# Splitting the ring of h: fifteen slots for loaded parts, six for rounded ones

## The chip, the cores and the metric

The kernel runs on one core of a Trainium2 chip. The metric is device time in microseconds (us) of one execution. The core has five engines, each with an instruction queue of its own that is worked in order: TensorE (PE, with its weight loads as PEld), VectorE (DVE), ScalarE (ACT), GpSimd (POOL) and SyncE (SP), which here only issues DMA transfers. An instruction that waits for a semaphore holds up everything behind it on its engine.

## The reference

A retention layer gives x, and a mixture of eight experts with dense weights is applied to it. Cut to the core:

```python
def _attn_ref(q, k, v):                       # 4 x 8 heads, 768 steps, 64 wide
    for t in range(S):
        state = gamma[None, :, None, None] * state + einsum('bhd,bhe->bhde', k[:, :, t], v[:, :, t])
        y[:, :, t] = scale * einsum('bhd,bhde->bhe', q[:, :, t], state)

def _moe_ref(x, w_gate, w1, w2):              # x: 3072 x 512, 8 experts, F = 1024
    logits = x @ w_gate
    P = exp(logits - logits.max())
    for _ in range(8):
        P /= P.sum(1, keepdims=True) + 1e-09
        P /= P.sum(0, keepdims=True) + 1e-09
        P *= N / E
    for e in range(E):
        h = maximum(x @ w1[e], 0.0)
        out += P[:, e:e + 1] * (h @ w2[e])
```

All arrays are float32.

## The kernel before, in words

The products of the experts are done with Strassen's scheme at one level, in the form that needs seven products M1 to M7 for a 2 by 2 block product. Each float32 operand is split into two parts that TensorE takes at full rate: a rounded value ("hi", made by ScalarE, `hi_act`, line 77) and the remainder ("lo", a subtraction on VectorE or GpSimd, line 80). A product is then three matmuls: hi x hi, lo x hi, hi x lo.

Three pieces of work follow one another.

*Retention* (up to about 145 us) gives x, written to `xd` in device memory.

*Stage 1* (x @ w1, matmuls on line 190) is 96 units of class `UnitA`: 32 pieces of w1 by three pieces of x. A unit is seven products of six matmuls. The loop goes through the units by `ROW`, seven places m = 0 to 6: M6 of unit n, M1 of n+1, M3 and M7 of n, M2 and M5 of n+1, M4 of n. `post` takes each product out of PSUM (lines 207 to 229), and the seven combinations of h that stage 2 needs (after the relu) are stored to `hd` (line 200). Line 213 is M3's sum on VectorE; M5 of the next unit uses the same PSUM bank and waits for it. Below, row 94 and row 95 are the last two turns of this loop (`n == NUA - 2` and `n == NUA - 1`). Units 93, 94 and 95 are the last users of three buffers of split w1, `WA`, each 7 slots of 512 columns.

*Stage 2* (h @ w2, matmuls on line 540) is 24 units of class `UnitB`: eight experts by three pieces of x. A product is cut into four quarters, so there are 24 x 7 x 4 = 672 parts, numbered s. Part s needs one piece of 128 x 512 of h: `h_load(s)` loads it from `hd` on SyncE's queue (line 600), `h_conv(s)` splits it (ScalarE rounds, VectorE subtracts in place, lines 605 and 606), and `b_part(s)` issues its six matmuls, then the work that follows the product (`post`, on every fourth part), a load, the split of part s+5 and, on three parts of four, one task from a list that prepares the next expert's w2 (`w2_tasks`: four subtractions on GpSimd on line 641, three roundings, three remainders, twice for each expert). M2, M3, M7 and M4 end in `emit` (lines 549 to 558): VectorE combines and scales the output, and a DMA takes it out; from the second expert on GpSimd issues that DMA, which adds to `out`.

The loaded and split parts live in a ring `HR` in the three `WA` buffers, which are free by then: nine slots of 1024 columns, the first half for hi, the second for the loaded value, which becomes lo. Part s uses slot s % 9:

```python
HR = [WA[(len(jobs) - 3 + k) % 3]....[:, i * 1024:(i + 1) * 1024]
      .rearrange("p (h t) -> p h t", h=2) for k in range(3) for i in range(3)]
```

In stage 2 `b_part(s)` issues the load of part s+9 behind the matmuls of part s, which free its slot. At the change of stage the loads of parts 0 to 2 stand at the start of row 94, those of 3 to 5 at the start of row 95, and those of 6 to 8 behind unit 95; `b_part(4)` adds those of 9 to 12. Parts 0 to 3 are computed inside row 95: 0 and 1 behind M6, 2 and 3 behind M7.

The order on each engine is the order in which the program issues the instructions; there is no planner.

Of the kernel before, what the change touches and what calls it, by code (L numbers as in the profile page):

```python
# [18 lines left out]
P = 128  # L19
# [18 lines left out]
M1, M2, M3, M4, M5, M6, M7 = range(7)  # L38
# [3 lines left out]
XP = {M1: 0, M2: 1, M3: 2, M7: 3, M5: 4, M6: 5, M4: 6}  # L42
# [5 lines left out]
def kernel(  # L48
# [17 lines left out]
    pe, act, dve, pool = nc.tensor, nc.scalar, nc.vector, nc.gpsimd  # L66
    sp = nc.sync
# [5 lines left out]
    def rd(t):  # L73
        return t.bitcast(F32)

    def hi_act(o, i):
        act.activation(o, i, AF.Copy)  # L77

    def lo(eng, o, full, h):
        eng.tensor_tensor(o, full, rd(h), ALU.subtract)  # L80
# [14 lines left out]
    X0 = cst.tile([P, 7, 2, 1024], F32R, name="X0")  # L95
    WA = [cst.tile([P, 7, 2, 256], F32R, name=f"WA{i}") for i in range(2)]
# [4 lines left out]
    hd = [[[drp.tile([P, QE, 512], F32, name=f"hd{e}_{r}_{i}") for i in range(7)] for r in range(NPAIR)] for e in range(E)]  # L101
    pd = drp.tile([NTILE * E, P], F32, name="pd")

    def run(q, n):
        for _ in range(min(n, len(q))):
            q.pop(0)()


    def x_load(t, r):
        for i, c, d in ((M1, 0, 0), (M7, 1, 0), (M3, 1, 1), (M2, 0, 1)):  # L110
            for k in range(2):
                sp.dma_start(rd(t[:, XP[i], 1, k * 512:(k + 1) * 512]).rearrange("p (b s) -> p b s", s=C),  # L112
                             xd[2 * r + c][:, :, 2 * d + k, :])
# [37 lines left out]
    def w1_load(n):  # L151
        sp.dma_start(w1_raw(n)[:, 0:4, :], w1[jobs[n]])
# [26 lines left out]
    class UnitA:  # L179
# [5 lines left out]
        def mm(self, i):  # L185
            ps = PS1[self.bank[i]]
            w, x = WA[self.job % 3][:, WP[i]], self.x[:, XP[i]]
            for k in range(2):
                for m, (a, b) in enumerate(((0, 0), (1, 0), (0, 1))):
                    pe.matmul(ps, w[:, a, k * P:(k + 1) * P], x[:, b, k * 512:(k + 1) * 512],  # L190
                              start=i in PRE and k == 0 and m == 0, stop=k == 1 and m == 2, **kw)
# [55 lines left out]
    jobs, first, last = {}, {}, {}  # L247
# [6 lines left out]
    with tc.manual_schedule():  # L254
        with ExitStack() as ph:
# [156 lines left out]
            for tau in range(2, NCHUNK):  # L412
                c, b = divmod(tau, B)
# [80 lines left out]
        def sink_t():  # L494
# [15 lines left out]
        NUA = len(UA)  # L510


        HR = [WA[(len(jobs) - 3 + k) % 3].rearrange("p s h c -> p (s h c)")[:, i * 1024:(i + 1) * 1024]
              .rearrange("p (h t) -> p h t", h=2) for k in range(3) for i in range(3)]
        NSH = len(HR)
        WB = [X1, X0]
        YS = [OT[:, 10:12, :], XSC[:, 0:2, :], XSC[:, 2:4, :]]
        TB = [OT[:, 2 * k:2 * k + 2, :] for k in range(3)]
# [3 lines left out]
        class UnitB:  # L522
# [12 lines left out]
            def mm(self, i, q, h):  # L535
                ps = self.bank(i)
                w = WB[(E - 1 - self.e) % 2][:, VP[i]]
                for d in range(2):
                    for m, (a, b) in enumerate(((0, 0), (1, 0), (0, 1))):
                        pe.matmul(ps[d] if isinstance(ps, tuple) else ps[:, d, :], w[:, a, q * 256 + d * P:q * 256 + d * P + P], h[:, b, :],  # L540
                                  start=i in PRE and q == 0 and m == 0, stop=q == QE - 1 and m == 2, **kw)

            def emit(self, c, dh, src, add):
# [53 lines left out]
        def h_load(s):  # L597
            if s < len(parts):
                u, i, q = parts[s]
                sp.dma_start(rd(HR[s % NSH][:, 1]), hd[u.e][u.r][i][:, q, :])  # L600

        def h_conv(s):
            if s < len(parts):
                t = HR[s % NSH]
                hi_act(t[:, 0], rd(t[:, 1]))
                lo(dve, t[:, 1], rd(t[:, 1]), t[:, 0])

        w2x = RW.rearrange("p (s c) -> p s c", s=7)

# [46 lines left out]

        bq = []

        def b_part(s):
            u, i, q = parts[s]  # L660
            if i == M6 and q == 0 and u.n + 1 < len(UB):
                UB[u.n + 1].load_p()
            u.mm(i, q, HR[s % NSH])
            if q == QE - 1:
                u.post(i)
            if s == 4:
                for x in range(NSH, NSH + 4):
                    h_load(x)
            if s >= 4:
                h_load(s + NSH)  # L670
                h_conv(s + 5)
            e, g = divmod(u.n, NPAIR)
            if q != 1:
                run(bq, 1)
            if g == 0 and i == M6 and q == 0 and e + 1 < E:
                bq.extend(w2_tasks(e + 1, 0) + w2_tasks(e + 1, 1))
# [13 lines left out]
        for n, u in enumerate(UA):  # L690
            v = UA[n + 1] if n + 1 < NUA else None
            while conv < loaded and n >= first[conv] - 2 and n > last.get(conv - 3, -1):
                wq += w1_tasks(conv, pool, dve)
                conv += 1
            if n == NJ:
                x_load(X0, 2)
                xq = x_tasks(X0, [dve, pool])
            if n == 40:
                ps_s.close()
                ps_B = ctx.enter_context(tc.tile_pool(name="ps_B", bufs=1, space=PSUM, reuse_waits="tile"))  # L700
                PS2 = [ps_B.tile([P, 2, 512], F32, name=f"psB{i}") for i in range(2)]
            if n == NUA - 2:
                UB[0].load_p()
            if n >= NUA - 2:
                for s in range(3):
                    h_load(s + 3 * (n - NUA + 2))
            for m, (k, i) in enumerate(ROW):
                w = (u, v)[k]
                if w is not None:
                    w.mm(i)  # L710
                    w.post(i)
                if m == 0 and carry is not None:
                    carry.last_sum()
                if m == 4:
                    u.sums()
                if m in (0, 1, 5):
                    run(wq, 1)
                if m in (1, 6) or n >= NJ:
                    run(xq, 2 if n >= NJ else 1)
                for f, x in w2_plan.get((n, m), ()):  # L720
                    w2_first(f, x)
                if n == NUA - 2 and m in (1, 3, 6):
                    h_conv((1, 3, 6).index(m))
                if n == NUA - 1 and m in (0, 1):
                    h_conv(3 + m)
                if n == NUA - 1 and m in (0, 3):
                    b_part(0 if m == 0 else 2)
                    b_part(1 if m == 0 else 3)
            carry = u
            while loaded < len(jobs) and loaded <= conv + 1 and n + 1 >= first[loaded] - 3:  # L730
                w1_load(loaded)
                loaded += 1
            if 12 <= n < 12 + len(sink):
                sink[n - 12]()
        carry.last_sum()
        for s in range(6, NSH):
            h_load(s)
        for s in range(5, NSH):
            h_conv(s)
        for s in range(4, len(parts)):  # L740
            b_part(s)
# [51 lines left out]
```

## Time and profile before

| | |
|---|---|
| median of 3 runs | 2132.11 us (2131.82 to 2138.85) |
| the profiled execution | 2132.21 us |
| its span, first to last instruction | 2129.5 us |
| PE busy | 2015.4 us, 95% of the span |
| DVE, ACT, POOL busy | 1543.6, 1041.1, 497.3 us |
| mean granted TensorE clock | 0.982 |
| parts of h: loads | 672 of 256 KB, median 5.7 us from issue to landing |
| moved by DMA | 503.62 MB, mean 236 GB/s |

The profile is of one execution. A line of the timeline gives the start and length in us, the engine (SPq for a DMA that SyncE issues), the program's line, the operation, out<-in by the program's names, shapes, the count, and in brackets how long the engine had been idle and what ended that. A line of the groups gives busy time and mean ns, then the idle time before the group and its releasers. A line of the stretches gives the bounds, the length, the busy time with the count, the granted clock, the DMA engines' busy share and GB/s. The chain of waits is the work that ended last, followed back, each piece with start and length. Matmul ends are modelled: a matmul's record is longer than its share of the pipeline, so a pause on TensorE is better counted from the number of matmuls in a stretch than from idle time.

### The profile page before, as it was taken

The numbers are of one execution on the slowest core, as the hardware profiler recorded it, in microseconds if no ns is written. First come the engines' busy times: TensorE is split into PE (matmuls) and PEld (weight loads), VectorE is DVE, ScalarE is ACT, GpSimd is POOL, SyncE is SP. The second block draws the span as 40 slices with busy tenths as digits, with TensorE's granted clock in tenths as the row PEclk, the third lists the DMA queues.
The fourth block names the chain that finished last, engine by engine and source line by source line (L and its number), as shares of the span: only waits on it lengthen the run. The fifth ranks groups of instructions, "written<-read, shape, count | busy, mean of one in ns | idle before, by whom it ended". The sixth has DMA issues, their size and how long they took to land.

```text
span 2129.5 us, 28865 instructions
## 1 busy us (share of the span) xinstructions
PE 2015.4 (95%) x9273; PEld 1646.9 (77%) x9273; DVE 1543.6 (72%) x2025; ACT 1041.1 (49%) x1668; POOL 497.3 (23%) x479
## 2 busy tenths in 40 slices
PE   7788999998999999999998999999999999999997
PEld 6786877886788888888876777877878787777886
DVE  6795988986566666666665777779587777768765
ACT  3343554553444444444444545555464555555553
POOL 4462433332121111211221201212030212203001
PEclk9899999999999999999998999999999999999999
DMA  7755776775566666666666778999989999989987
GB/s 231 242 168 178 251 228 225 242 238 176 201 224 227 218 219 216 227 223 220 231 231 233 241 254 255 275 268 250 282 247 261 271 256 271 261 268 247 261 261 180
DMA packets 252906, 503.62 MB, mean 236 GB/s; under 512 B 27793, under 2 KB 40401, under 8 KB 250705
## 3 DMA queue, kind: packets, MB, share of 16 engines
q1 hardware_dynamic: 240656, 457.73, 63.9%
q0 software_dynamic: 12096, 44.05, 12.1%
q8 instruction: 72, 1.18, 0.2%
q14 instruction: 82, 0.66, 0.1%
HBM read 268.79 MB, written 232.88 MB: 236 GB/s over the span
## 4 chain that ended last, share of the span: by engine, by line
PE 65%; DVE 13%; DMA 10%; issue 7%; ACT 3%; SPq 1%; POOL 1%; DVEq 0%; POOLq 0%; ACTq 0%
PE psA L190 41%; PE psA L540 12%; PE psB L540 10%; DMA WA<-hd 7%; DVE WA L80 6%; DVE X L80 2%; DVE XSC L551 1%; ACT WA L77 1%; DVE QL L80 1%; DMA raw<-kT 1%; SPq L112 1%; PE ps_s L327 1%; DVE OT L551 1%; DMA RW<-w 1%; DVE ta L330 0%
## 5 line engine op out<-in xcount | busy, mean ns | idle before, releaser
L190 PE MATMUL psA<-X,WA 128*128 128x512 f32 x4032 | 939.1, 395 | 29.3 <-DVE OT L213 20.3
L190 PEld LDWEIGHTS psA<-X,WA 128*128 128x128 f32 x4032 | 766.0, 191 | 197.5 <-DVE OT L213 22.8
L80 DVE TENSOR_TENSOR WA<-WA 128x512 fp32r<-128x512 f32 x672 | 489.0, 769 | 243.4 <-ACT WA L77 242.9
L77 ACT ACTIVATE WA<-WA 128x512 fp32r<-128x512 f32 x672 | 408.3, 631 | 429.3 <-DMA WA<-hd 365.5
L540 PE MATMUL psA<-WA,X 128*128 128x512 f32 x2304 | 544.5, 392 | 23.2 <-DVE WA L80 19.8
L540 PEld LDWEIGHTS psA<-WA,X 128*128 128x128 f32 x2304 | 428.8, 188 | 129.6 <-DVE WA L80 34.6
L540 PE MATMUL psB<-WA,X 128*128 128x512 f32 x1728 | 416.1, 395 | 17.5 <-DVE WA L80 11.7
L540 PEld LDWEIGHTS psB<-WA,X 128*128 128x128 f32 x1728 | 325.7, 190 | 98.5 <-DVE WA L80 25.1
L158 POOL TENSOR_TENSOR RW<-RW 128x256 f32<-128x256 f32 x244 | 225.8, 935 | 634.0 <-DMA RW<-w 404.8
L80 DVE TENSOR_TENSOR WA<-RW,WA 128x768 fp32r<-128x768 f32 x122 | 146.4, 1200 | 53.3 <-ACT WA L77 53.2
L219 ACT ACTIVATE OT<-OT 128x512 f32<-128x512 f32 x96 | 60.9, 634 | 240.7 <-DVE OT L218 240.7
L558 POOL DMA_DIRECT2D out<-XSC x57 | 49.5, 868 | 509.9 <-DVE XSC L553 405.2
L213 DVE TENSOR_TENSOR OT<-psA,OT 128x512 f32<-128x512 f32 x96 | 66.2, 689 | 105.2 <-PE psA L190 105.1
L77 ACT ACTIVATE WA<-RW 128x768 fp32r<-128x768 f32 x122 | 109.7, 948 | 21.2 <-POOL RW L158 13.9
L225 DVE TENSOR_TENSOR OT<-psA,OT 128x512 f32<-128x512 f32 x96 | 66.3, 690 | 59.0 <-ACT OT L219 50.7
L641 POOL TENSOR_TENSOR RW<-RW 128x512 f32<-128x512 f32 x56 | 89.3, 1600 | 67.7 <-DMA RW<-w 65.6
L236 DVE TENSOR_TENSOR OT<-OT 128x512 f32<-128x512 f32 x96 | 91.5, 953 | 3.3
L229 ACT ACTIVATE OT<-psA 128x512 f32<-128x512 f32 x96 | 57.6, 600 | 73.5 <-PE psA L190 46.8
L226 ACT ACTIVATE OT<-OT 128x512 f32<-128x512 f32 x96 | 61.0, 635 | 66.1 <-DVE OT L225 66.1
L240 DVE TENSOR_TENSOR OT<-OT 128x512 f32<-128x512 f32 x96 | 69.1, 720 | 30.8 <-ACT OT L229 26.9
L211 ACT ACTIVATE OT<-psA 128x512 f32<-128x512 f32 x96 | 57.5, 599 | 67.9 <-PE psA L190 67.9
L558 POOL DMA_DIRECT2D out<-OT x27 | 23.4, 866 | 240.6 <-DVE OT L553 176.9
(109 smaller groups left out, 1450.8 us busy)
## 6 DMA issues: line engine op xcount, KB each, us to landing
hd<-OT SPq DMA_DIRECT2D x672, 256.0 KB, 2.6
WA<-hd SPq DMA_DIRECT2D x672, 256.0 KB, 5.7
RW<-w SPq DMA_DIRECT2D x61, 512.0 KB, 4.4
out<-XSC POOLq DMA_DIRECT2D x57, 512.0 KB, 8.0
RW<-w SPq DMA_DIRECT2D x16, 1024.0 KB, 8.4
out<-OT POOLq DMA_DIRECT2D x27, 512.0 KB, 8.0
OT<-pd SPq DMA_DIRECT2D x23, 512.0 KB, 6.4
raw<-kT SPq DMA_DIRECT2D x24, 256.0 KB, 3.9
```

The source lines that it names most:

```text
L77: act.activation(o, i, AF.Copy)
L80: eng.tensor_tensor(o, full, rd(h), ALU.subtract)
L158: eng_add.tensor_tensor(x[:, WP[o]], x[:, WP[p]], x[:, WP[q]], op)
L190: pe.matmul(ps, w[:, a, k * P:(k + 1) * P], x[:, b, k * 512:(k + 1) * 512], start=i in PRE and k == 0 and m == 0, stop=k == 1 and m == 2, ...
L213: dve.tensor_tensor(c12, ps, u2, ALU.add)
L225: dve.tensor_tensor(o, ps, s1, ALU.add)
L226: act.activation(o, o, AF.Relu)
L236: dve.tensor_tensor(t["S2"], t["S1"], t["A11"], ALU.subtract)
L240: dve.tensor_tensor(self.new("S4"), self.t["A12"], self.t["S2"], ALU.subtract)
L540: pe.matmul(ps[d] if isinstance(ps, tuple) else ps[:, d, :], w[:, a, q * 256 + d * P:q * 256 + d * P + P], h[:, b, :], start=i in PRE and ...
L558: pool.dma_start(o, y.rearrange("p d t -> p (d t)"), accum_op=ALU.add)
L641: return lambda: pool.tensor_tensor(w2x[:, VP[o]], w2x[:, VP[a]], w2x[:, VP[b]], ALU.subtract)
```

## The change

The ring of h is parted in two. A `WA` buffer holds seven slots of 512 columns; of the 21 slots six become `HH`, for rounded values (part s in slot s % 6), and fifteen become `HL`, for loaded values, which become remainders in place. Parts 8 to 11 use four further places in X0's M1 (`HX`), free since M1 of unit 95, until the second expert's w2 is put there.

```diff
+        ring = [[WA[(len(jobs) - 3 + k) % 3].rearrange("p s h c -> p (s h c)")[:, i * 512:(i + 1) * 512] for i in range(7)]
+                for k in range(3)]
+        HH = ring[0][4:] + ring[1][4:]
+        HL = ring[0][:4] + ring[1][:4] + ring[2]
+        NHH, NHL = len(HH), len(HL)
+        HX = [X0[:, XP[M1], k // 2, (k % 2) * 512:(k % 2 + 1) * 512] for k in range(4)]
+
+        def place(s):
+            return HX[s - 8] if 8 <= s < 12 else HL[(s if s < 8 else s - 4) % NHL]
+
+        def follows(s):
+            u = s - 4 - NHL
+            return u if u < 8 else u + 4
...
-                sp.dma_start(rd(HR[s % NSH][:, 1]), hd[u.e][u.r][i][:, q, :])
+                sp.dma_start(rd(place(s)), hd[u.e][u.r][i][:, q, :])
...
-                t = HR[s % NSH]
-                hi_act(t[:, 0], rd(t[:, 1]))
-                lo(dve, t[:, 1], rd(t[:, 1]), t[:, 0])
+                hi, low = HH[s % NHH], place(s)
+                hi_act(hi, rd(low))
+                lo(dve, low, rd(low), hi)
...
+        nload = [NHL + 4]
...
-            if s == 4:
-                for x in range(NSH, NSH + 4):
-                    h_load(x)
             if s >= 4:
-                h_load(s + NSH)
+                while follows(nload[0]) <= s:
+                    h_load(nload[0])
+                    nload[0] += 1
                 h_conv(s + 5)
...
             if n >= NUA - 2:
-                for s in range(3):
-                    h_load(s + 3 * (n - NUA + 2))
+                for s in (range(4) if n == NUA - 2 else range(4, 12)):
+                    h_load(s)
...
-                if n == NUA - 2 and m in (1, 3, 6):
-                    h_conv((1, 3, 6).index(m))
-                if n == NUA - 1 and m in (0, 1):
-                    h_conv(3 + m)
-                if n == NUA - 1 and m in (0, 3):
-                    b_part(0 if m == 0 else 2)
-                    b_part(1 if m == 0 else 3)
+                if n == NUA - 2 and m in (5, 6):
+                    h_conv(m - 5)
+                if n == NUA - 1:
+                    for x in {1: (0, 1), 4: (2, 3)}.get(m, ()):
+                        b_part(x)
+                    for x in {1: (2,), 3: (3,), 4: (4,), 5: (5,)}.get(m, ()):
+                        h_conv(x)
...
-        for s in range(6, NSH):
+        for s in range(12, NHL + 4):
             h_load(s)
-        for s in range(5, NSH):
+        for s in range(6, 9):
             h_conv(s)
```

In steady state the load of a part is issued behind the matmuls of the part fifteen before it, and a rounding must wait for the matmuls of the part six before it. The split of part s+5 still stands behind the matmuls of part s. At the change of stage four loads stand at the start of row 94, eight at the start of row 95, and parts 12 to 18 behind unit 95. The splits of parts 0 and 1 move from places 1 and 3 of row 94 to places 5 and 6, that of part 2 from place 6 of row 94 to place 1 of row 95, that of part 3 from place 0 to 3, that of part 4 from place 1 to 4, and that of part 5 from behind the loop to place 5. In row 95 no product of a next unit is left at places 1, 4 and 5, so the matmuls of parts 0 to 3 keep their order on TensorE: 0 and 1 behind M6, 2 and 3 behind M7.

More of the change, by code (lines that the diff above doesn't have):

```diff
@@ L510 @@
         NUA = len(UA)
-        HR = [WA[(len(jobs) - 3 + k) % 3].rearrange("p s h c -> p (s h c)")[:, i * 1024:(i + 1) * 1024]
-              .rearrange("p (h t) -> p h t", h=2) for k in range(3) for i in range(3)]
-        NSH = len(HR)
+        ring = [[WA[(len(jobs) - 3 + k) % 3].rearrange("p s h c -> p (s h c)")[:, i * 512:(i + 1) * 512] for i in range(7)]
[9 more added lines that the diff above has]
+            return u if u < 8 else u + 4
         WB = [X1, X0]
@@ L539, in mm @@
                     for m, (a, b) in enumerate(((0, 0), (1, 0), (0, 1))):
-                        pe.matmul(ps[d] if isinstance(ps, tuple) else ps[:, d, :], w[:, a, q * 256 + d * P:q * 256 + d * P + P], h[:, b, :],
+                        pe.matmul(ps[d] if isinstance(ps, tuple) else ps[:, d, :], w[:, a, q * 256 + d * P:q * 256 + d * P + P], h[b],
                                   start=i in PRE and q == 0 and m == 0, stop=q == QE - 1 and m == 2, **kw)
@@ L662, in b_part @@
                 UB[u.n + 1].load_p()
-            u.mm(i, q, HR[s % NSH])
+            u.mm(i, q, (HH[s % NHH], place(s)))
             if q == QE - 1:
                 u.post(i)
-            if s == 4:
-                for x in range(NSH, NSH + 4):
-                    h_load(x)
             if s >= 4:
-                h_load(s + NSH)
+                while follows(nload[0]) <= s:
+                    h_load(nload[0])
+                    nload[0] += 1
                 h_conv(s + 5)
```

## The prediction

> **What bounds the kernel now.** I read the waits first, then the matmul timeline at the change of stage, then counted matmuls in stretches of stage 2.
>
> ```profile
> span 2129.5 us, 28865 instructions
> L77 ACT ACTIVATE WA<-WA 128x512 fp32r<-128x512 f32 x672 | 408.3, 631 | 429.3 <-DMA WA<-hd 365.5
> SPq L600 <- PE psA L540: 288.6, 309, 1.2
> 1262.31 10.88 PE psB L540 x48
> 1153.80:2118.90 965.10, 927.88 (x3985) 1.00 0.90 259
> 1116.60:1153.80 37.20, 25.49 (x84) 0.82 0.66 217
> ```
>
> Row 2 (groups of instructions): ScalarE spends 365.5 us waiting for parts of h to land. Row 3 (SyncE's own waits): their loads wait for matmuls, because a slot of the ring must be read empty first. So loads are asked for late, not slowly. Row 4 (chain of waits) is a stretch with nothing in the way: 48 matmuls in 10.88 us, 0.2267 us each, 1.36 us for a part of six. The last two rows (busy time by stretch; PE with its count, granted clock, DMA share, GB/s) hold what can be won. From part 8 to the last matmul, 3985 matmuls would need 903.4 us and took 965.1: 61.7 us lost. At the change of stage 84 would need 19.0 us and took 37.2: 18.2 lost. The pool is 80 us. Everything before 1116 us runs the same instructions in the same order, and so does the tail after the last matmul.
>
> **Change of stage.** TensorE, then the engines around it, in order of time:
>
> ```profile
> 1099.72 16.81 PE L190 MATMUL psA<-X,WA 128*128 128x512 f32 x72
> 1121.73 6.34 PE L190 MATMUL psA<-X,WA 128*128 128x512 f32 x18 [5.21 <-DVE OT L213]
> 1139.36 2.73 PE L190 MATMUL psA<-X,WA 128*128 128x512 f32 x6 [3.06 <-DVE OT L218]
> 1149.12 4.87 PE L540 MATMUL psB<-WA,X 128*128 128x512 f32 x12 [3.03 <-ACT WA L77]
> 1119.72 0.63 ACT L77 ACTIVATE WA<-WA 128x512 fp32r<-128x512 f32 x1 [6.58 <-DMA WA<-hd]
> 1133.69 0.63 ACT L77 ACTIVATE WA<-WA 128x512 fp32r<-128x512 f32 x1 [3.61 <-DMA WA<-hd]
> 1151.01 5.42 ACT L77 ACTIVATE WA<-WA 128x512 fp32r<-128x512 f32 x8 [1.20 <-DMA WA<-hd]
> 1120.38 0.69 DVE L80 TENSOR_TENSOR WA<-WA 128x512 fp32r<-128x512 f32 x1 [8.53 <-ACT WA L77]
> 1112.26 1.56 SPq L600 DMA_DIRECT2D WA<-hd  x3
> 1128.47 1.66 SPq L600 DMA_DIRECT2D WA<-hd  x3
> 1144.68 7.59 SPq L600 DMA_DIRECT2D WA<-hd  x10
> ```
>
> Part 0's split is queued on ScalarE and VectorE in the middle of unit 94's row. VectorE stands 8.53 us in front of it, because part 0 was asked for at 1112.26 and ScalarE could round it only at 1119.72, when it had landed. Behind it on VectorE is M3's sum (L213), and for that sum TensorE waits 5.21 us. The same happens with parts 3 to 5, asked for at 1128.47, and with part 6, asked for at 1144.68.
>
> **The edits, in order of time.**
>
> (1) Four loads instead of three before row 94, at the same place of SyncE's queue: still 1112.26, the fourth 0.5 us later (1.56 for three). Part 0 still lands at 1119.7.
>
> (2) The splits of parts 0 and 1 move behind M5 and M4 of row 94, so L213 no longer stands behind them. The 18 matmuls, which are M5, M4 and then M6 of unit 95, follow the 72 without a break, from 1116.4 to 1120.5 (18 x 0.2267). Part 0's rounding ends at 1120.35, its remainder 0.69 later: 0.25 us late for the third matmul. ScalarE then has M4's relu, one w2 rounding and part 1's rounding; at 0.63 each (the row of 1119.72) that ends near 1122.2, and TensorE waits 0.4 in part 1. M3 and M7 of unit 95 follow (2.72), to 1126.6. Part 3's rounding is queued behind M7's relu, and that behind M7's sum on VectorE: sum 0.69 (as at 1120.38), relu, w2 rounding and part 3's own at 0.63 each, and some 0.5 of hand-offs and of VectorE's work ahead of the sum, 3.1 after M7's end. Part 2 covers 1.36 of it less the overlap: 1.9 late, plus 0.35 for the remainder. The four waits make 2.9 us.
>
> (3) Eight loads (parts 4 to 11) instead of three go out before row 95. SyncE reaches them when M4's relu is stored, about 1121.3, and they take 8 x 0.5 = 4 us. Landing as the loads of 1128.47 did (5.2 us to 1133.69) and at most 0.68 apart (eight roundings that follow the landings in 5.42, row 1151.01), parts 4 to 11 are there from 1126.6 to 1131.3; part 4 can start at 1133.1. Parts 8 to 11 use X0's M1, whose last matmul ran at 1112. Behind these loads on SyncE are unit 95's stores, 4 us later; their buffers are not written again before the first copies of stage 2, some 20 us on. I take 0, at most +1.
>
> (4) Parts 12 to 18 are loaded behind the last stores, about 1135, land from 1140 and are wanted at 1144 and later.
>
> The loss of 18.2 becomes 2.9: **15.3 us gained**, between 18.2 (no wait left) and 8 (the load's wait lands on M4's copy and costs the two other waits, 3.06 and 3.03, and their slow matmuls again).
>
> (5) Loads run 15 parts ahead, not 9: 6 x 1.36 = 8.2 us more. There are 672 of them as before, so their price on SyncE is 0. The chain of waits shows its longest landing, before the last burst, which is now covered by about 20 us of lead:
>
> ```profile
> 1898.08 12.31 DMA WA<-hd
> ```
>
> (6) Rounded values have six slots, not nine. Part s+5's rounding now waits until part s-1 is through: a new wait on ScalarE. Behind it are the w2 roundings and the copies of part s+1, which need a later matmul anyway. From there to the part's third matmul are 5 x 1.36 - 0.17 + 0.45 = 7.1 us, and rounding, remainder and hand-offs take 1.4. The 5.7 us over must hold what stands ahead on VectorE. Price 0; see the third rival.
>
> **What (5) is worth.** Six stretches of 32 us and one of 36, around the preparation of the next expert's w2, beside a whole one of 32:
>
> ```profile
> 1374.00:1406.00 32.00, 32.00 (x143) 1.00 0.91 260
> 1169.00:1205.00 36.00, 33.07 (x135) 0.95 0.70 229
> 1298.00:1330.00 32.00, 27.84 (x114) 1.00 0.89 239
> 1420.00:1452.00 32.00, 27.92 (x117) 1.00 0.88 234
> 1542.00:1574.00 32.00, 27.82 (x114) 1.00 0.89 233
> 1663.00:1695.00 32.00, 28.12 (x118) 1.00 0.88 232
> 1784.00:1816.00 32.00, 28.04 (x117) 1.00 0.89 241
> 1906.00:1938.00 32.00, 25.98 (x104) 0.95 0.84 234
> ```
>
> Against 143 the six miss 29, 26, 29, 25, 26 and 39 matmuls: 39.5 us. The first misses 25.8 of 160.8: 5.9. So 45.4 of the 61.7 us lie in seven bursts. The one at 1420, by VectorE, with M3's end on TensorE ahead of it and GpSimd beside it:
>
> ```profile
> 1417.74 4.92 PE L540 MATMUL psA<-WA,X 128*128 128x512 f32 x21
> 1422.02 2.73 DVE L80 TENSOR_TENSOR WA<-WA 128x512 fp32r<-128x512 f32 x4 [2.51 <-ACT WA L77]
> 1424.67 1.28 DVE L551 TENSOR_TENSOR XSC<-psA,OT 128x512 f32<-128x512 f32 x2
> 1427.13 6.52 DVE L80 TENSOR_TENSOR WA<-WA 128x512 fp32r<-128x512 f32 x4
> 1433.57 1.21 DVE L551 TENSOR_TENSOR XSC<-psB,OT 128x1024 f32<-128x1024 f32 x1
> 1435.96 4.35 DVE L80 TENSOR_TENSOR WA<-WA 128x512 fp32r<-128x512 f32 x4
> 1440.24 1.74 DVE L80 TENSOR_TENSOR X<-RW,X 128x1536 fp32r<-128x1536 f32 x1
> 1444.29 1.29 DVE L80 TENSOR_TENSOR WA<-WA 128x512 fp32r<-128x512 f32 x2
> 1428.07 5.03 POOL L641 TENSOR_TENSOR RW<-RW 128x512 f32<-128x512 f32 x3
> 1452.00:1542.00 90.00, 89.52 (x393) 1.00 0.96 274
> ```
>
> M3 ends at 1422.66. Its output (L551) starts at 1424.67, because VectorE is still at four remainders that landed late (idle 2.51 before them). From there VectorE has no pause until part 204's remainder: 1424.67 to 1444.29 is 19.6 us, with the remainder 20.3. TensorE needs 12 parts less the overlap, 16.6 us, to reach the matmul that wants it. The chain alone costs 20.3 - 16.6 = 3.7, and its late start of 2.0 makes 5.7, as counted (26 x 0.2267 = 5.9). With loads 8.2 us earlier the four remainders are done before M3 ends, the chain starts at once, and 3.7 stays. Seven bursts keep 25.9 of 45.4: **19.5 gained**. Bounds: 0, if something else delays the chain; 45.4, if it fits.
>
> What makes the chain long is in it: four remainders take 6.44 us there (1427.13 to 1433.57), against 2.73 at 1422.02, while GpSimd runs its three subtractions. GpSimd is released by the output just before, so both move together, and I keep the 6.44. The Trainium skill ("SBUF — State Buffer", "Who interferes with whom") says that a VectorE instruction with two SBUF inputs and a GpSimd instruction that reads SBUF exclude each other for the whole instruction. By that rule 3.7 us stays per burst, as here; if the slowdown did not follow GpSimd, four remainders at 2.73 would take 3.7 off and nothing would stay, which is the second rival's time. The trace agrees with the rule in this place (6.44 beside 5.03 of GpSimd).
>
> Outside the bursts 61.7 - 45.4 = 16.3 us are lost in small stalls. I count as staying those by VectorE's order, once per expert behind the second half of w2, and the last unit's end:
>
> ```profile
> 1478.00 6.05 PE L540 MATMUL psA<-WA,X 128*128 128x512 f32 x26
> 1484.50 5.29 PE L540 MATMUL psA<-WA,X 128*128 128x512 f32 x22 [0.45 <-DVE WA L80]
> 1489.63 2.65 PE L540 MATMUL psB<-WA,X 128*128 128x512 f32 x11
> 2113.22 5.69 PE L540 MATMUL psA<-WA,X 128*128 128x512 f32 x24 [2.23 <-DVE XSC L551]
> ```
>
> From 1478.00 to 1489.63 are 48 matmuls, 10.88 us of work in 11.63: 0.75, six times 4.5. With the 2.23 at the end, behind an output, that leaves **9 gained**, between 0 and 16.
>
> Sum: 15.3 + 19.5 + 9 = 44. The profiled execution took 2132.2 us (span 2129.5 and 2.7 around it; the median is 2132.1). 2132 - 44 = **2088 us**.
>
> **Rivals.** *Only the change of stage gains* (0.17). The loads come earlier, but VectorE's order or the transfers keep stage 2 as it is: 2132 - 15 = 2117. For it: DMA share 0.96 between bursts, so little room. Against it: that stretch (last row of the burst's fence) already does 393 matmuls in 90 us, 99% of full speed, at that share.
>
> *The bursts dissolve* (0.07): VectorE works five parts ahead and the chain never reaches TensorE: another 26 off, 2062. Against it: M7's and M2's outputs stand in the chain and can't run before their matmuls.
>
> *Six slots are too few* (0.05), the other sign. If what stands on VectorE ahead of a remainder exceeds the 5.7 us of (6), TensorE stalls. The longest such piece in the rows is 1440.24 to 1444.29, 4.05 us, and with a w2 rounding on ScalarE 5.5: inside by 0.2. Were each of the 96 outputs (4 per unit, 24 units) to cost 0.6 us over it, 57 us would be lost: 2146. It decides from 0.45 us each.
>
> *No effect* (0.05): what is gained at the change of stage is waited for later, since VectorE sets the pace of the first units: 2132.
>
> **Numbers.** Forecast 0.66, 2080 to 2100 on its own. Half a per cent, 11 us, is about what a measurement of this kernel can tell from no change. Faster: the forecast and the first two rivals, 0.90; same 0.05; slower 0.05. The range leaves out the last two rivals and the far end of the second: 2074 to 2117.
>
> **What would show it.** The 5.21 before unit 95's M5 is gone and part 8 starts near 1138.5, not 1153.8. ScalarE's wait for loads falls from 365.5 to under 100 us, and its wait for matmuls grows by as much. L551 behind M3 starts within 0.3 us of M3's end in the bursts, and these 32 us hold some 126 matmuls (143 less 3.7 / 0.2267). If L551 still starts 2 us late, step (5) is wrong; if ScalarE's wait for matmuls is followed by TensorE waiting for roundings throughout stage 2, step (6) is.

## The result, and the profile after

The changed kernel takes 2080.51 us (median of 4, 2077.7 to 2083.44) against 2133.43 us (median of 4, 2131.82 to 2138.85): a ratio of 0.975, with a 95% interval of 0.973 to 0.9771, some 53 us. The profiled execution took 2079.61 us, against 2132.21 before. The forecast was 2088, in a range of 2074 to 2117.

First the profile of the changed kernel: its span, the group of ScalarE's roundings, and from the view of the waits what ScalarE's roundings and copies and SyncE's loads wait for (us in total, times, longest; SyncE's row from 1260 us on, as in the prediction). Line 540 is now 551, 551 is 562, 553 is 564, 558 is 569, 568 is 579, 587 is 598, 600 is 611, 611 is 622, 615 is 626 and 641 is 652.

```profile
span 2077.1 us, 28831 instructions
L77 ACT ACTIVATE WA<-WA 128x512 fp32r<-128x512 f32 x668 | 402.4, 629 | 256.4 <-PE psB L551 109.9
ACT WA L77 <- DMA WA<-hd: 2.4, 2, 1.7
ACT WA L77 <- PE psB L551: 109.9, 169, 1.3
ACT WA L77 <- PE psA L551: 107.8, 161, 1.3
ACT OT L579 <- PE psA L551: 69.3, 48, 1.6
ACT OT L579 <- PE psB L551: 53.2, 23, 2.3
SPq L611 <- PE psA L551: 277.2, 301, 2.3
```

ScalarE's wait for parts of h fell from 365.5 us to 2.4. ScalarE isn't busier: it waits now for matmuls of stage 2, 340.2 us in these four rows. The same four rows of the kernel before hold 40.1:

```profile
ACT WA L77 <- PE psB L540: 12.4, 8, 4.7
ACT WA L77 <- PE psA L540: 11.3, 10, 3.4
ACT OT L568 <- PE psA L540: 9.8, 16, 2.4
ACT OT L568 <- PE psB L540: 6.6, 7, 1.7
```

So 363 us of waiting for loads became 300 us of waiting for TensorE, and most of the rest is the 52.4 us by which the span is shorter. SyncE's loads still wait for matmuls as before (277.2 us, where 288.6 were); that wait is not the harm by itself.

Then busy time by stretch, PE with its count, granted clock, DMA share, GB/s: the change of stage, part 8 to the last matmul, the first expert's preparation of w2, and the first and last of six stretches around that of the later experts (the four between have 127 or 128 matmuls too).

```profile
1115.40:1142.55 27.15, 22.49 (x85) 0.87 0.84 291
1142.55:2066.00 923.45, 908.38 (x3984) 1.00 0.92 270
1153.00:1189.00 36.00, 36.00 (x160) 1.00 0.89 292
1276.00:1308.00 32.00, 29.46 (x127) 1.00 0.92 251
1863.00:1895.00 32.00, 29.54 (x128) 1.00 0.93 259
```

By lengths: the change of stage is 10.05 us shorter (37.20 to 27.15), stage 2 from part 8 on is 41.65 shorter (965.10 to 923.45), stage 1 ended 1.2 sooner, and the tail is 0.5 longer: 52.4, the difference of the spans. By what is still lost at 0.2267 us for a matmul: 7.9 us at the change of stage (27.15 less 85 x 0.2267), where 18.2 were; 20.3 in stage 2 (923.45 less 3984 x 0.2267), where 61.7 were. The six stretches miss 15 or 16 matmuls of 143, some 3.5 us each and 20.9 in all: that is everything stage 2 still loses. The first expert's preparation loses nothing (160 in 36 us), and the small stalls between the bursts are gone.

The change of stage on TensorE, and the stretch of part 3's and M4's matmuls:

```profile
1120.93 2.89 PE L551 MATMUL psB<-WA,X 128*128 128x512 f32 x10 [0.88 <-DVE WA L80]
1127.72 1.19 PE L551 MATMUL psB<-WA,X 128*128 128x512 f32 x4 [0.71 <-DVE WA L80]
1131.95 2.93 PE L551 MATMUL psB<-WA,X 128*128 128x512 f32 x6 [3.04 <-ACT WA L77]
1134.67 2.58 PE L190 MATMUL psA<-X,WA 128*128 128x512 f32 x6
1131.95:1137.10 5.15, 5.15 (x13) 0.52 0.49 185
```

The 5.21 us in front of M5 are gone. Part 8 starts at 1142.55, not at the 1138.5 foretold: there are three pauses, for the remainders of parts 0 and 2 and for part 3's rounding, and after the longest the six matmuls of part 3 and M4's six take 5.15 us from start to start, where twelve at the full rate take 2.72. The granted clock of these 5.15 us is 0.52 (last row; 0.87 in the whole stretch). What stands behind the pauses, on VectorE, ScalarE and GpSimd:

```profile
1119.30 3.27 DVE L80 TENSOR_TENSOR WA<-WA 128x512 fp32r<-128x512 f32 x2
1122.49 1.78 DVE L240 TENSOR_TENSOR OT<-OT 128x512 f32<-128x512 f32 x1
1124.19 1.77 DVE L80 TENSOR_TENSOR X<-RW,X 128x512 fp32r<-128x512 f32 x1
1125.89 1.78 DVE L80 TENSOR_TENSOR WA<-WA 128x512 fp32r<-128x512 f32 x1
1127.59 0.68 DVE L213 TENSOR_TENSOR OT<-psA,OT 128x512 f32<-128x512 f32 x1
1131.28 0.61 ACT L77 ACTIVATE WA<-WA 128x512 fp32r<-128x512 f32 x1
1116.82 6.90 POOL L626 TENSOR_TENSOR RW<-RW 128x512 f32<-128x512 f32 x4 [4.98 <-DVE OT L234]
1123.68 3.44 POOL L80 TENSOR_TENSOR X<-RW,X 128x512 fp32r<-128x512 f32 x2
```

From 1116.82 to 1127.1 GpSimd works without a break (four subtractions of the first w2, then two of its remainders), and the five VectorE steps that start from 1119.30 on take 1.6 to 1.8 us each, 8.3 us in all, where 0.69 each would make 3.5 (the one before them, at 1117.97, took 1.20). The next, at 1127.59, takes 0.68. M3's sum (L213) stands behind them, M7's sum and relu behind that, and part 3's rounding, queued behind the relu, runs only at 1131.28.

A burst of stage 2, at the place in the code that the prediction showed at 1420, on VectorE and GpSimd; the last row is GpSimd in the first expert:

```profile
1392.13 2.70 DVE L80 TENSOR_TENSOR WA<-WA,WA 128x512 fp32r<-128x512 f32 x4 [2.52 <-ACT WA L77]
1395.74 1.37 DVE L562 TENSOR_TENSOR XSC<-psA,OT 128x512 f32<-128x512 f32 x2 [0.91 <-PE psA L551]
1398.29 4.82 DVE L80 TENSOR_TENSOR WA<-WA,WA 128x512 fp32r<-128x512 f32 x3
1403.03 1.78 DVE L80 TENSOR_TENSOR WA<-WA 128x512 fp32r<-128x512 f32 x1
1398.66 0.86 POOL L569 DMA_DIRECT2D out<-XSC  x1 [16.72 <-DMA WA<-hd]
1399.23 5.03 POOL L652 TENSOR_TENSOR RW<-RW 128x512 f32<-128x512 f32 x3
1163.09 6.61 POOL L652 TENSOR_TENSOR RW<-RW 128x512 f32<-128x512 f32 x4 [29.25 <-DVE WA L80]
```

The four remainders ahead of M3's output are done when VectorE starts to wait (0.91 us, for TensorE): the output starts as soon as M3 ends, not 2 us later. Behind it four remainders still take 6.5 us beside GpSimd's three subtractions. GpSimd starts those at 1399.23, behind the output that it issues itself (fifth and sixth row; VectorE has finished the output's data at 1398.37, 0.3 us before GpSimd issues it, so the 16.72 put down to a load is most likely the wait for that output). In the first expert, where SyncE issues the outputs, nothing stands ahead of the subtractions on GpSimd: they start at 1163.09 (last row), 0.74 us ahead of M3's output at 1163.83, all four in a row, and there TensorE loses nothing: the four remainders behind the output take 4.7 us. In the later bursts the fourth subtraction comes behind the next output, at 1408.12, and two more remainders there take 3.15 us. That the output's place on GpSimd makes the difference is argued from these times; no run moved the output alone.

### The profile page after: what moved, and what is told of

Read it like the earlier page. It is cut to its first block, busy times and chain, and to the rows that moved or that the text cites. A ratio compares the mean times of both kernels' runs of the same rounds, so it can differ in the third digit from the quotient of the medians.

```text
span 2077.1 us, 28831 instructions
## 1 busy us (share of the span) xinstructions
PE 1992.0 (96%) x9273; PEld 1647.7 (79%) x9273; DVE 1549.1 (75%) x2025; ACT 1042.0 (50%) x1668; POOL 499.5 (24%) x479
## 4 chain that ended last, share of the span: by engine, by line
PE 81%; DVE 6%; issue 5%; DMA 5%; SPq 1%; ACT 1%; POOL 0%; POOLq 0%; DVEq 0%; ACTq 0%
PE psA L190 41%; PE psA L551 21%; PE psB L551 16%; DMA WA<-hd 3%; DVE WA L80 2%; DVE QL L80 1%; PE ps_s L327 1%; SPq L112 1%; DVE X L80 1%; PE ps_x L363 1%; DMA RW<-w 1%; PE psA L372 1%; PE ps_t L339 1%; PE ps_x L358 1%; DVE ta L330 0%
## 5 line engine op out<-in xcount | busy, mean ns | idle before, releaser
L190 PE MATMUL psA<-X,WA 128*128 128x512 f32 x4032 | 932.2, 393 | 23.8 <-DVE OT L213 18.2
L190 PEld LDWEIGHTS psA<-X,WA 128*128 128x128 f32 x4032 | 762.4, 190 | 188.9 <-DVE OT L213 20.3
L551 PE MATMUL psA<-WA,X 128*128 128x512 f32 x2296 | 535.9, 390 | 10.6 <-DVE WA L80 10.1
L77 ACT ACTIVATE WA<-WA 128x512 fp32r<-128x512 f32 x668 | 402.4, 629 | 256.4 <-PE psB L551 109.9
L80 DVE TENSOR_TENSOR WA<-WA,WA 128x512 fp32r<-128x512 f32 x487 | 352.3, 767 | 103.4 <-ACT WA L77 97.4
L551 PE MATMUL psB<-WA,X 128*128 128x512 f32 x1728 | 405.1, 390 | 9.1 <-DVE WA L80 6.1
L80 DVE TENSOR_TENSOR WA<-RW,WA 128x768 fp32r<-128x768 f32 x122 | 145.3, 1192 | 52.6 <-ACT WA L77 52.3
L80 DVE TENSOR_TENSOR WA<-WA 128x512 fp32r<-128x512 f32 x181 | 138.8, 794 | 36.9 <-ACT WA L77 35.1
L213 DVE TENSOR_TENSOR OT<-psA,OT 128x512 f32<-128x512 f32 x96 | 66.2, 690 | 106.8 <-PE psA L190 106.8
```

The costliest lines, as they stand in the source:

```text
L213: dve.tensor_tensor(c12, ps, u2, ALU.add)
```

## The experiments

### What carried the gain: the layout, the distance or the slots

**The new order at the change of stage alone**, in the kernel before, with its ring of nine:

```diff
-                if n == NUA - 2 and m in (1, 3, 6):
-                    h_conv((1, 3, 6).index(m))
-                if n == NUA - 1 and m in (0, 1):
-                    h_conv(3 + m)
-                if n == NUA - 1 and m in (0, 3):
-                    b_part(0 if m == 0 else 2)
-                    b_part(1 if m == 0 else 3)
+                if n == NUA - 2 and m in (5, 6):
+                    h_conv(m - 5)
+                if n == NUA - 1:
+                    for x in {1: (0, 1), 4: (2, 3)}.get(m, ()):
+                        b_part(x)
+                    for x in {1: (2,), 3: (3,), 4: (4,), 5: (5,)}.get(m, ()):
+                        h_conv(x)
...
-        for s in range(5, NSH):
+        for s in range(6, NSH):
```

> The old ring of nine slots with the new places of the splits at the change of stage alone (parts 0 and 1 behind M5 and M4 of row 94, part 2 behind parts 0 and 1, and so on); loads as before. Theory A (the two halves of the change add up: about 10 us at the change of stage, about 41 us from loads that run 15 parts ahead): the wait of 5.21 us for L213 goes, the loads of parts 3 to 8 stay as late as before, so at most 8 us are won, about 2126; the pauses from part 8 on stay at some 60 us. Rival B (the stalls of stage 2 come from how stage 2 is entered, and a good start removes them): near 2085.

Measured: 2125.87 us against 2132.53, ratio 0.9969 (0.9952 to 0.9986): 6.7 us. Stretches of this kernel (change of stage, part 8 to the end) and the matmuls of part 6:

```profile
1115.50:1147.76 32.26, 23.99 (x82) 0.84 0.72 245
1147.76:2113.00 965.24, 926.84 (x3984) 1.00 0.90 259
1143.36 4.61 PE L540 MATMUL psB<-WA,X 128*128 128x512 f32 x12 [3.65 <-ACT WA L77]
```

The change of stage is 5 us shorter; part 6 waits 3.65 us, since its load is still asked for late. Stage 2 is as before, to 0.2 us. So the order of the splits is a minor share of the gain, and a better start does not speed up the steady state. The rival *Only the change of stage gains* is out already by the changed kernel's own stretches, where stage 2 gains 41.65 us.

**The two rings, with the loads of stage 2 issued nine parts ahead** in the program, as in the old ring:

```diff
-                while follows(nload[0]) <= s:
+                while max(follows(nload[0]), nload[0] - 9) <= s:
```

> The changed kernel, but in stage 2 the load of part s is issued only behind part s-9, as in the old ring; rings, start and splits as changed. Theory A: the stalls of stage 2 come back almost whole, 30 to 41 us, 2111 to 2121, and L562 behind M3 starts 1 to 2 us late again in the bursts. Rival B (the start is what matters) and rival C (the separation of rounded and loaded values itself frees slots, not the distance of the loads): 2081, as the changed kernel.

**The same with twelve parts ahead**:

```diff
-                while follows(nload[0]) <= s:
+                while max(follows(nload[0]), nload[0] - 12) <= s:
```

> The changed kernel with each load of stage 2 issued behind the part twelve before it, instead of fifteen (nine gave 2114.0). Theory A (a load must be out ahead of its rounding by its landing, which takes 5.7 us in the middle and up to 12.3): twelve parts are 16.3 us, less the 8 us that the split stands ahead, so most landings fit and few do not: 2080 to 2090. If the gain grew evenly with the distance, it would be halfway, 2097.

Measured: 9 ahead 2113.98 us, ratio 0.9901 (0.9877 to 0.9925); 12 ahead 2080.56, ratio 0.9769 (0.9744 to 0.9794). With "9 ahead" stage 2 loses 55 us (960.00 less 3990 x 0.2267, first row) and ScalarE waits 145.3 us for loads (second row); with "12 ahead" that wait is 17.4 us (third row). The last two rows are SyncE's waits with "9 ahead", for the loads of the output's scales (L598) and of w2 (L622).

```profile
1140.00:2100.00 960.00, 924.46 (x3990) 1.00 0.88 261
ACT WA L77 <- DMA WA<-hd: 145.3, 60, 6.9
ACT WA L77 <- DMA WA<-hd: 17.4, 13, 2.9
SPq L598 <- DVE XSC L560: 89.6, 13, 10.0
SPq L622 <- DVE X L80: 79.1, 7, 13.2
```

The edits do not hold the loads at nine and twelve parts. They set a load's place in SyncE's queue; what a load waits for is still its slot, and with fifteen slots that is free long before. Taking the loads and the matmuls of each trace in order (parts 19 to 671), a load starts this long before its part's first matmul:

| run | median, us | shortest, us | roundings within 0.3 us of the landing | lost in stage 2, us |
|---|---|---|---|---|
| layout alone (ring of nine) | 10.7 | 5.5 | 464 of 653 | 62 |
| two rings, "9 ahead" | 15.0 | 5.3 | 198 | 55 |
| two rings, "12 ahead" | 18.9 | 9.6 | 62 | 22 |
| the changed kernel | 18.9 | 13.5 | 0 | 20 |

Of the 198 loads that ScalarE still has to wait for with "9 ahead", 60 lie in the first expert, whose outputs also leave by SyncE's queue; the other 138 are all among the first twelve behind an L598 or L622, which wait for VectorE (89.6 and 79.1 us; 15.0 and 0.2 in the changed kernel). SyncE's loads also wait 116.5 us for landings there, 8.2 in the changed kernel; what these waits are was not traced. So the lead of the loads carries the gain in stage 2: with the same rings and the same splits, the kernel with the late loads is 30 us slower than "12 ahead" (28 by the ratios, 33 by the medians), and "12 ahead", whose loads have the same median lead as the changed kernel's, cannot be told from it. How the time goes with the lead in between was not measured. An estimate fits: a part is split five parts ahead of its matmuls, 6.8 us, which leaves 3.9 of 10.7 us for a landing whose median is 5.7, and 12.1 of 18.9.

**Five slots for rounded parts instead of six**:

```diff
-        HH = ring[0][4:] + ring[1][4:]
+        HH = (ring[0][4:] + ring[1][4:])[:5]
```

> The changed kernel with five slots for rounded values instead of six: a rounding waits for the part five before it, 1.36 us later than with six. Theory A (six slots cost nothing, there is 5.7 us to spare in front of a remainder): five cost little, 0 to 1 us for each of six bursts, 2080 to 2087. Rival E (six slots are already at the edge): each of the 96 outputs costs 0.5 us or more, 2125 or more.

Measured: 2082.51 us, ratio 0.9758 (0.9742 to 0.9774), not to be told from the changed kernel's. Its burst at 1400 holds 127 matmuls in 32 us. A slot fewer costs at most a couple of us. The rival *Six slots are too few* is out, with room to spare.

### What the bursts still lose

**The subtractions of w2 in stage 2 left out**:

```diff
-            q += [tt(*x) for x in w2t]
+            q += [lambda: None] * 4
```

> The changed kernel without GpSimd's four subtractions in the preparation of the next expert's w2 (left out: so the combinations of w2 for the second to eighth expert are not formed). Theory A (what is left in each burst, 3.4 us six times, is VectorE's chain, made longer by GpSimd's subtractions, 4.0 us of slowed remainders): the bursts go, 20 us less, about 2060; four remainders behind M3's output take 2.7 us instead of 6.5. Rival D (the chain is too long by the outputs and the w2 remainders, whatever GpSimd does): within 5 us of the changed kernel, 2076 to 2081.

Measured: 2059.19 us, ratio 0.9659 (0.9635 to 0.9682), some 20 us under the changed kernel. Stage 2, the place of a burst, and VectorE in it:

```profile
1135.00:2043.00 908.00, 907.51 (x4003) 1.00 0.93 276
1377.00:1409.00 32.00, 32.00 (x143) 1.00 0.98 283
1391.34 1.89 DVE L80 TENSOR_TENSOR WA<-WA,WA 128x512 fp32r<-128x512 f32 x3
1393.14 0.69 DVE L80 TENSOR_TENSOR WA<-WA 128x512 fp32r<-128x512 f32 x1
```

The four remainders behind M3's output take 2.5 us instead of 6.5, and no burst is left: stage 2 loses 0.5 us. The 20.3 us that the changed kernel loses hang on GpSimd's subtractions. Leaving them out also frees w2's roundings from waiting for them, so this experiment alone doesn't part the two; the remainders' own time fell by 4.0 us, more than the 3.5 of a burst. The second row shows too that TensorE runs at the full rate with the DMA engines 98% busy: the transfers are not the bound.

**The subtractions three places earlier**:

```diff
-            q = [lambda: w2_load(e, f)] + [lambda: None] * 6
+            q = [lambda: w2_load(e, f)] + [lambda: None] * 3
```

> The changed kernel with three empty places instead of six between the load of w2 and GpSimd's four subtractions, so that three of the four are issued ahead of M3's output instead of behind it. Theory A: the slowed remainders move in front of the output, where VectorE has five parts in hand, and the bursts shrink from 3.4 us to 0 to 1.5: 2061 to 2070. Rival D (total work of VectorE around there is what is too much, wherever the subtractions stand): 2077 to 2081.

Measured: 2071.08 us, ratio 0.9717 (0.9699 to 0.9735). Faster by some 7 to 9 us, just short of the range that was expected. GpSimd and the first three remainders behind the output, in the burst:

```profile
1394.10 4.91 POOL L652 TENSOR_TENSOR RW<-RW 128x512 f32<-128x512 f32 x3 [13.07 <-DMA RW<-w]
1397.77 4.53 DVE L80 TENSOR_TENSOR WA<-WA,WA 128x512 fp32r<-128x512 f32 x3
```

The subtractions got only partly ahead. M3's output starts at 1394.82; they start 0.7 us ahead of it, where in the changed kernel they start 3.5 us behind it (1399.23 and 1395.74), and no sooner because GpSimd had stood 13.07 us for w2 to land. So they run beside the output and the first two of the four remainders, and the four take 5.1 us where they took 6.5. w2's own first remainder moved up as well, ahead of the next output. A burst still costs about 2 us (134 matmuls of 143).

**Split seven parts ahead instead of five**, with eight slots for rounded parts and thirteen for loaded ones:

```diff
-        HH = ring[0][4:] + ring[1][4:]
-        HL = ring[0][:4] + ring[1][:4] + ring[2]
+        HH = ring[0][4:] + ring[1][4:] + ring[2][5:]
+        HL = ring[0][:4] + ring[1][:4] + ring[2][:5]
...
-                h_conv(s + 5)
+                h_conv(s + 7)
...
-        for s in range(6, 9):
+        for s in range(6, 11):
```

> The changed kernel with eight slots for rounded and thirteen for loaded parts, and each split issued seven parts ahead instead of five. Theory A: two more remainders stand ahead of M3's output on VectorE, so the chain from there to the remainder that TensorE wants is shorter by two of them and TensorE comes 2.7 us later; by the rows about 1 us is left of the 3.4 of each burst: 2064 to 2069. Loads 13 ahead still cover the longest landing. Rival G (thirteen loaded slots are too few): some of the small stalls come back, over 2080.

Measured: 2069.39 us, ratio 0.9707 (0.9688 to 0.9726). Two parts of lead take 9 to 11 us off. The bursts keep 1.1 to 2.8 us each, most of them more than the 1 us expected (135 matmuls of 143 in the one at 1400).

**The load and the subtractions of w2's first half one unit earlier** (with part 3's split one place earlier, as in the last but one experiment below):

```diff
-                bq.extend(w2_tasks(e + 1, 0) + w2_tasks(e + 1, 1))
+                bq.extend(w2_tasks(e + 1, 0)[11 if e else 0:] + w2_tasks(e + 1, 1))
+            if g == 2 and i == M6 and q == 0 and e + 2 < E:
+                bq.extend(w2_tasks(e + 2, 0)[:11])
```

> The changed kernel with part 3's split behind M3 of row 95, and with the load of the first half of the next expert's w2 and GpSimd's four subtractions on it one unit (28 parts, 38 us) earlier, since they only need the raw buffer, which is free by then; the roundings and remainders stay where they were, from the third expert on. Theory A (the bursts are GpSimd's subtractions slowing VectorE's remainders between two outputs): the five bursts from the third expert on go, 17 us, and 3 us at the change of stage: about 2060. Rival D (the outputs and the w2 remainders alone are too much there): 2072 to 2078; and if the slowed remainders only move, new pauses one unit earlier, 2075.

**Both**, the seven parts ahead and the unit earlier:

> The same with eight slots for rounded and thirteen for loaded parts and the splits seven parts ahead. Theory A: the last of the bursts (the second expert's, and what VectorE's order leaves) goes too; 2056 to 2060, within 3 us of the other. Rival G (the added waits for thirteen slots): over 2064.

Measured: the unit earlier 2066.79 us, ratio 0.9708 (0.9687 to 0.9728); both 2061.84 (2058.61 to 2064.68) against 2130.34, ratio 0.9682 (0.9664 to 0.97). Of the unit earlier, the place of the old burst and the place to which the subtractions went; of both, all of stage 2:

```profile
1393.00:1425.00 32.00, 32.00 (x143) 1.00 0.87 257
1358.00:1390.00 32.00, 30.98 (x135) 1.00 0.98 262
```

```profile
1134.70:2046.00 911.30, 909.92 (x4003) 1.00 0.93 275
```

The old bursts are empty, so what remained of them did hang on where the subtractions stand. But the slow steps of VectorE went along with the subtractions and cost some 1.7 us at the new place: 2060 was expected and missed. With seven parts of lead as well, stage 2 loses 3.8 us in all (911.30 less 4003 x 0.2267). This is the fastest kernel here that leaves no work out, 15 us under the changed kernel by the ratios and 19 by the medians. In it ScalarE waits 127.1 us for loads again (thirteen slots, split seven ahead), and TensorE does not notice.

### The change of stage

**Part 3 split one place earlier**:

```diff
-                    for x in {1: (2,), 3: (3,), 4: (4,), 5: (5,)}.get(m, ()):
+                    for x in {1: (2,), 2: (3,), 4: (4,), 5: (5,)}.get(m, ()):
```

> The changed kernel with one move: the split of part 3 stands behind M3 of row 95 instead of behind M7. Theory A (part 3's wait at the change of stage comes from its rounding being queued behind M7's relu, and that behind VectorE's queue, which GpSimd's subtractions slow down): the 3.04 us pause of TensorE before part 3's rounding shrinks to about 1, some 3 us less in all, 2077 to 2078; stage 2 stays. Rival F (what is lost there is the slower clock after the pause and the late landing, whatever the order): no pause gone, 2080.

Measured: 2077.78 us, ratio 0.975 (0.973 to 0.9771), the changed kernel's own ratio. The 3.04 us in front of part 3 went; pauses of about 1 us each came in front of part 4's rounding and of its remainder, and this one stands in front of part 0's remainder:

```profile
1120.08 3.78 PE L551 MATMUL psB<-WA,X 128*128 128x512 f32 x10 [2.02 <-DVE WA L80]
```

That last pause is not of the edit's making: part 0's split stands ahead of the edit in every queue, and the kernel with five rounded slots, which has the old order, shows 1.98 us at the same place (0.88 in the changed kernel). It differs from execution to execution, since GpSimd's subtractions start now just after a VectorE step (0.04 us, changed kernel) and now just ahead of it (0.29 us, five slots), which then takes 1.67 us instead of 0.69. From part 0's first matmul to part 8's are 21.6 us here, where the changed kernel takes 23.2 and the six other runs with its order 22.9 to 23.8. The two other kernels with part 3 moved (the unit earlier, and both) take 22.6 and 21.7. So the order of ScalarE's queue makes the pause in front of part 3, but only a microsecond or so of the way.

**Row 94's four subtractions of w2 left out**:

```diff
-            w2_plan[NUA - 2, x + 2] = [(1, w2t[x])]
+            pass
```

> The changed kernel without GpSimd's four subtractions in row 94 (left out: so the second half of the first expert's w2 lacks its combinations). What failed in the forecast is the change of stage: 8.1 us of pauses are left there, 2.9 were forecast. Theory H (the forecast took 0.69 us for each VectorE step; GpSimd's subtractions, 1116.8 to 1123.7, stretch several to 1.7 to 1.8 and so push M7's sum, its relu and part 3's rounding back): without them the steps take 0.69, part 3's rounding comes some 4 us earlier, the 3.04 us pause before it shrinks to 1 or less, 2075 to 2077. Rival I (the order of ScalarE's queue alone holds part 3): pause of 2 us or more, 2079 to 2081.

Measured: 2074.9 us (2070.21 to 2076.66) against 2131.2, ratio 0.9729 (0.9711 to 0.9747). The intervals of the two ratios overlap; the traces say more. VectorE and TensorE of this kernel:

```profile
1127.57 0.68 DVE L218 TENSOR_TENSOR OT<-psA,OT 128x512 f32<-128x512 f32 x1
1130.01 2.00 PE L551 MATMUL psB<-WA,X 128*128 128x512 f32 x6 [1.84 <-ACT WA L77]
1131.84 1.53 PE L190 MATMUL psA<-X,WA 128*128 128x512 f32 x6
1139.49 0.61 PE L551 MATMUL psA<-WA,X 128*128 128x512 f32 x2
```

Most of VectorE's steps are back at 0.69, M7's sum (L218) starts 0.9 us after M7's end where it started 3.1 after it, the pause ahead of part 3 falls from 3.04 to 1.84, M4's six matmuls from 2.58 to 1.53, and the granted clock stays at 1.00 behind the pause. From the last matmul ahead of part 0 to part 8 the way is 19.8 us instead of 23.1. So GpSimd's subtractions make 3.3 of the 5 us by which the loss exceeded the forecast (7.9 against 2.9). The 1.84 that stays lies between the two theories: the one that put the pause down to the subtractions alone expected at most 1, the one that put it down to the order of the queues at least 2. It is what the prediction itself had for part 3's wait without slowed steps, 1.9. Two VectorE steps here still take 1.77 and 1.78 us, beside GpSimd's remainders of w2, which were left in; what these add wasn't tried.

## Why the prediction was right, and where it was off

The time came out 7.5 us under the forecast, inside its own range of 2080 to 2100, and the mechanism was the one forecast: the loads were asked for too late, and distance mends it. By its terms (gained, forecast and measured): change of stage 15.3 and 10.3; bursts 19.5 and 24.5; small stalls 9 and 16; sum 44 and 51, with 1.2 at the end of stage 1 and the longer tail not forecast at all. The errors had opposite signs, 5 us too much at the change of stage and 12 too little in stage 2, so part of the closeness is luck.

- **The loads' distance (5)**: right. The median lead grew by 8.2 us, as worked out (10.7 to 18.9). The two signs foretold are there: M3's output starts when M3 ends, and the bursts hold 127 or 128 matmuls, where some 126 were foretold. That some 3.7 us would remain, by VectorE's remainders beside GpSimd, is borne out (3.5 measured; gone without the subtractions, though leaving them out frees w2's roundings too). Two sizes were off, both for the better. The bursts were counted as seven that cost 3.7 each, but the first expert's costs nothing. I had not seen that its outputs leave by SyncE, so that GpSimd's subtractions don't stand behind an output there. And stage 2's small stalls all went with the earlier loads; I had kept half of them as VectorE's order.
- **The splits at the change of stage (2)**: mis-sized, 7.9 us lost where "the four waits make 2.9". From start to start, parts 0 and 1 lose 1.6 us (0.25 and 0.4 forecast), the way through part 2 to part 3 loses 4.2 (1.9 forecast), and part 3 and M4 lose 2.4 (0.35 forecast, for the remainder); that makes 8.2, 0.3 more than the count over the whole stretch. The step that failed is "some 0.5 of hand-offs and of VectorE's work ahead of the sum": M7's sum starts 3.1 us after M7's end (1126.40, where part 2 begins, to 1129.51), while the sum itself takes 0.68, as forecast. VectorE was some 2.6 us late for M3's sum already, because GpSimd's subtractions and remainders had made the steps before it 1.6 to 1.8. The prediction weighed that very slowdown for the bursts (6.44 us beside GpSimd) and did not ask for it at the change of stage. The row from which it took its 0.69 (1120.38) gave no warning, though the same four subtractions ran then (1117.87 to 1123.89): that step began 0.1 us before one of them ended, and the next one took 1.65 us instead of 1.26. The rule that it quoted from the Trainium skill ("SBUF — State Buffer", "Who interferes with whom") agrees with these traces: remainders mostly at 1.6 to 1.8 us beside GpSimd, 0.6 to 0.7 without it, in stage 2 and at row 94. The 2.4 us of part 3 and M4 are the slow clock (0.52 granted), which the prediction had in the worse bound of its range ("their slow matmuls again") and left out of this sum.
- **Loads in row 95 (3), (4)**: right. ScalarE's waits for loads in the whole kernel are 2.4 us; none holds TensorE.
- **Six slots (6)**: right at 0; even five cost next to nothing.
- **The waits**: ScalarE's wait for loads is 2.4 us, under 100 as foretold, and its waits for matmuls grew by 300, which with the shorter span accounts for it.
- **The rivals**: *Only the change of stage gains* falls with the 41.65 us that stage 2 gained. *The bursts dissolve* holds for one burst of seven, the first expert's; its 2062 is reached only when VectorE is given more lead and the subtractions are moved (2061.8) or when they are left out (2059.2). *Six slots are too few* and *No effect* fall.

The two rings with "9 ahead" are 12 us better than the layout alone with the ring of nine (2113.98 and 2125.87). Of these, 5 lie at the change of stage (28.3 and 23.1 us from part 0 to part 8; the loads of parts 6 to 8 are early in one and late in the other) and 7 in stage 2 (62 and 55 lost), where most loads of the two rings run ahead of nine, as the table above shows.

What stays open: what the separate slots are worth by themselves, since no run held all loads of the two rings at nine; and how much of the loss at the change of stage hangs on GpSimd's remainders of w2.

## What to carry to other kernels

Give a ring of loads its lead in time, not in slots: count how many parts of work cover a landing under load, from the place where the value is first touched (with the split five parts, 6.8 us, ahead, a median lead of 10.7 us was too little and one of 18.9 enough). Read the lead from the trace: a load's place in the program is only its place in a queue, and what stands ahead of it there can hold it up. Where two values of one slot live for different times, part the ring, so that the short-lived one does not take the other's room. When the loads are on time, the next bound is the engine's queue with the longest run of work between two products; price its steps with what runs beside them, since here a VectorE subtraction cost 0.69 us alone and mostly 1.6 to 1.8 beside GpSimd. Then give that engine more lead, or move the neighbour, and look at where the neighbour goes.

## What was not expected of the hardware

- VectorE's 128x512 steps with both inputs in SBUF mostly took 1.6 to 1.8 us when GpSimd's subtractions ran beside them and 0.68 to 0.69 when not, and without those in stage 2 the kernel is some 20 us shorter. Sums that read one input from PSUM took 0.68 beside them too (before, 1120.99 and 1122.67).
- TensorE ran at its full rate through stretches with a DMA share of 0.93 to 0.98 (143 matmuls in 32 us at 0.98): a share near 1 is no sign that transfers bound the work.
- After a pause of 3.04 us TensorE's next twelve matmuls took 5.15 us, 0.43 each, at a granted clock of 0.52. After one of 1.84 us (row 94's subtractions left out) the granted clock stayed at 1.00. That is no threshold: behind pauses of 1.67 and 1.69 us in two other runs, which had had longer ones just before, it fell to 0.50 and 0.55.
